# Token-major attention numerators, resident weights and small interleaved steps in a four-layer linear-attention and gated-MLP kernel

## Chip, cores and metric

The kernel runs on one core of one Trainium2 chip. The metric is the device time of one execution in microseconds (us). A time is a median over several executions.

Engines are named as in the profile: PE is the tensor engine, DVE the vector engine, ACT the scalar engine, POOL the GpSimd engine. SP issues most of the transfers (DMA).

## The reference

Two residual layers, A (linear attention with a "hedgehog" feature map) and B (a gated MLP), are applied twice: A, B, A, B. All data are bf16. There are S = 2048 tokens of D = 512 features, H = 32 heads of 16 features, and a hidden width F = 1376.

```python
def _A_ref(x, wqkv, w_phi, wo):                      # called on layernorm(x)
    q, k, v = split_heads(x @ wqkv)                  # cut: reshape and transpose to (b, h, s, 16)
    pq = einsum("bhsd,hdf->bhsf", q, w_phi)
    pk = einsum("bhsd,hdf->bhsf", k, w_phi)
    phi_q = concatenate([softmax(pq), softmax(-pq)], axis=-1)
    phi_k = concatenate([softmax(pk), softmax(-pk)], axis=-1)
    kv  = einsum("bhsf,bhsd->bhfd", phi_k, v)
    z   = einsum("bhsf->bhf", phi_k)
    num = einsum("bhqf,bhfd->bhqd", phi_q, kv)
    den = einsum("bhqf,bhf->bhq", phi_q, z)[..., None] + 1e-6
    return merge_heads(num / den) @ wo

def _B_ref(x, W_gate, W_up, W_down):                 # called on layernorm(x)
    return (relu(x @ W_gate) * (x @ W_up)) @ W_down

x = x + _A_ref(layernorm(x), ...); x = x + _B_ref(layernorm(x), ...)
x = x + _A_ref(layernorm(x), ...); x = x + _B_ref(layernorm(x), ...)
```

The important fact is that `kv` and `z` are sums over all tokens. No token's attention output can be computed before the last token's K and V are in. Each A layer therefore has two phases, a K/V phase and a query phase, with a barrier between them.

## The kernel before

The kernel records its operations one by one with what each reads and writes. A list scheduler in the kernel's own Python code then fixes the order on each engine, using an assumed duration per operation, and puts in the semaphore waits. The order on the chip is static: an instruction that has to wait holds up all that stand behind it on the same engine. Tokens are handled in 16 tiles of 128, or in 4 slabs of 512.

The layers are recorded one after the other. In the attention the query side is kept feature-major (features on the partitions, 512 tokens in the columns). Softmax sums and denominators then lie across partitions, so the kernel gets them with many small matmuls, takes reciprocals on DVE, transposes them on PE and spreads them again over the partitions with broadcast matmuls. Long lines are cut at `[...]`.

```python
for st in range(NSLAB):                 # softmax sums of q: 32 small matmuls a slab, 32 columns each
    for tt in range(4):
        for sg in range(2):
            for c in range(NC):
                op("pe", [...] e.matmul(zqv[:, tt, sg, :], expq[:, st, c, sg, tt*128:(tt+1)*128], EC2[:, c, :], [...]
    [...]                               # reciprocal, ratio R (DVE), 4 transposes (PE), copy (DVE)
    for c in range(NC):                 # R spread over partitions by a matmul of 512 columns
        op("pe", [...] e.matmul(pb[bk][:], EC[:, c, :], RT_sb[:, st*512:(st+1)*512], [...]
        [...]                           # expqm = expq * R, on POOL or DVE
[...]                                   # the same again for the denominators: 32 small matmuls, rden, transposes
for st in range(NSLAB):
    for c in range(NC):
        op("pe", [...] e.matmul(pb[nb][:], kvbd[:, 0, c, :], expq[:, st, c, 0, :], [...]      # numerator
        op("pe", [...] e.matmul(pb[nb][:], kvbd[:, 1, c, :], expqm[:, st, c, :], [...]        # numerator
        op("pe", [...] e.matmul(pb[rbb][:], EC[:, c, :], rdenT_sb[:, st*512:(st+1)*512], [...]  # 1/den spread
        [...]                           # oT = numerator * rdenb, POOL or DVE
    for tt in range(4):                 # output projection, residual on DVE
        [...]
```

The block-diagonal `kvbd` holds the 16x16 `kv` blocks of 8 heads on its diagonal, for a group of 128 features. DVE makes it from the sums in PSUM with a mask, 128 columns at a time, read and written in the same order:

```python
kvv = pb[bk][:, 0:136].rearrange("p (h e) -> p h e", e=17)
op("dve", [...] e.tensor_tensor(kvbd[:, sg, c, :].rearrange("p (h d) -> p h d", d=16), kvv[:, :, 0:16],
                                EC2[:, 0, 0:8].unsqueeze(2).to_broadcast([P, 8, 16]), ALU.mult) [...]
```

`kvbd` holds the 16x16 `kv` blocks of 8 heads on its diagonal. In the K/V phase, `vhat = v * 1/sum(exp(k))` is made on POOL or DVE for each sign of the feature map. The gated layer loads its weights (4.2 MB) into a region that shares its place with `vhat`, so they are loaded once for each gated layer:

```python
def layer_B(li, my_ln, next_ln):
    dma("sp", [...] Wg[:] [...]); dma("sp", [...] Wu[:] [...]); dma("sp", [...] Wd [...])
    for st in range(NSLAB):
        for fc in range(NFC):           # 11 column steps: 4 gate and 4 up matmuls of 512 columns,
            [...]                       # relu on ACT, product on DVE with "up" read from PSUM
        for tt in range(4):             # down projection: 11 matmuls of 512 columns a tile
            [...]
```

The softmax here doesn't subtract the row's maximum and nothing guards it: scores larger than these inputs give would overflow.

Of the kernel before, what the change touches and what calls it, by code (L numbers as in the profile page):

```python
# [45 lines left out]
class Program:  # L46
    SYNC_LAT = 500.0
# [222 lines left out]


class KB:

    def __init__(self, nc, A_x, A_wqkv, A_w_phi, A_wo, B_W_gate, B_W_up, B_W_down, out,
                 nlayers=4, debug_outs=None, dve_vhat_tiles=(2, 5, 7, 10, 13, 15), resid_on_pool=False, ot_mode="half", expqm_mode="half", nr_iters=1, ln_pre_emit=False, rstd_mode="dve", yt_copy_act="half", wcopy_act=True,
                 window=(("sp", 64), ("act", 96), ("pe", 300), ("dve", 24), ("pool", 32)), sched_params=(("SYNC_LAT", 500.0), ("SAME_LAT", 600.0))):
        self.dve_vhat_tiles = tuple(dve_vhat_tiles)
        self.resid_on_pool = resid_on_pool
        self.ot_mode = ot_mode
        self.expqm_mode = expqm_mode  # L280
        self.nr_iters = nr_iters
        self.ln_pre_emit = ln_pre_emit
        self.rstd_mode = rstd_mode
        self.yt_copy_act = yt_copy_act
        self.wcopy_act = wcopy_act
        self.nc = nc
        self.prog = Program(nc, window=dict(window))
        sp = dict(sched_params) if sched_params else {}
        if "SYNC_LAT" in sp:
            self.prog.SYNC_LAT = sp["SYNC_LAT"]  # L290
        if "SAME_LAT" in sp:
            self.prog.SAME_LAT = sp["SAME_LAT"]
        if "DMA_BW" in sp:
            self.prog.DMA_BW = sp["DMA_BW"]
        if "DMA_FIXED" in sp:
            self.prog.DMA_FIXED = sp["DMA_FIXED"]
        if "DMA_GLOBAL_Q" in sp:
            self.prog.DMA_GLOBAL_Q = sp["DMA_GLOBAL_Q"]
        self.A_x, self.A_wqkv, self.A_w_phi, self.A_wo = A_x, A_wqkv, A_w_phi, A_wo
        self.B_W_gate, self.B_W_up, self.B_W_down, self.out = B_W_gate, B_W_up, B_W_down, out  # L300
        self.debug_outs = debug_outs or {}
        self.nlayers = nlayers
        B, S, D = A_x.shape
        assert B == 1 and D == 512 and S % 512 == 0
        self.S = S
        self.NT = S // 128
        self.NSLAB = S // 512
        self.D = 512
        self.NC = 4
        self.H = 32  # L310
        self.DH = 16
        self.HF = 512
        self.F = B_W_gate.shape[1]
        assert self.F == 1376
        self.NFC = 11
        self.FLAST = self.F - 10 * 128
        self.eps_ln = 1e-5
        self.eps_den = 1e-6

    def op(self, eng, fn, reads=(), writes=(), dur=100.0, name=""):  # L320
        return self.prog.op(eng, fn, reads, writes, dur, name)

    def dma(self, eng, fn, reads=(), writes=(), nbytes=0, name=""):
        return self.prog.dma(eng, fn, reads, writes, nbytes, name)

    def build(self):
        nc = self.nc
        S, NT, NSLAB, NC, NFC = self.S, self.NT, self.NSLAB, self.NC, self.NFC
        with ExitStack() as ctx:
            E = ctx.enter_context  # L330
            self.sems = {e: E(nc.semaphore(f"sem_{e}")) for e in ENG_NAMES}
            self.dsems = [E(nc.semaphore(f"dsem{i}")) for i in range(self.prog.n_dma_sems)]

            x_sb = E(nc.sbuf_tensor("x_sb", [P, NT, 512], BF16))
            yT = E(nc.sbuf_tensor("yT", [P, NC, S], BF16))
            wv = E(nc.sbuf_tensor("wv", [P, NC, 512], BF16))
            Wqp = E(nc.sbuf_tensor("Wqp", [P, NC, 512], BF16))
            Wkp = E(nc.sbuf_tensor("Wkp", [P, NC, 512], BF16))
            wo_sb = E(nc.sbuf_tensor("wo_sb", [P, NC, 512], BF16))
            BD = E(nc.sbuf_tensor("BD", [P, NC, 128], BF16))  # L340
            ones_c = E(nc.sbuf_tensor("ones_c", [P, 4, 32], BF16))
            ident = E(nc.sbuf_tensor("ident", [P, 128], BF16))
            ident32 = E(nc.sbuf_tensor("ident32", [P, 128], FP32))
            EC2 = E(nc.sbuf_tensor("EC2", [P, 4, 32], BF16))
            EC2t = E(nc.sbuf_tensor("EC2t", [P, 4, 32], BF16))
            ones32 = E(nc.sbuf_tensor("ones32", [P, 4, 128], BF16))
            EC = E(nc.sbuf_tensor("EC", [P, 4, 128], BF16))
            eps_c = E(nc.sbuf_tensor("eps_c", [P, 1], FP32))
            stats6 = E(nc.sbuf_tensor("stats6", [P, NT, 6], FP32))
            mv = E(nc.sbuf_tensor("mv", [P, NT, 2], FP32))  # L350
            rstd = E(nc.sbuf_tensor("rstd", [P, NT, 1], FP32))
            rs_v1 = E(nc.sbuf_tensor("rs_v1", [P, NT, 1], FP32))
            rs_hx = E(nc.sbuf_tensor("rs_hx", [P, NT, 1], FP32))
# [45 lines left out]
            def RR(key):  # L399
                r = R.get(key)  # L400
                if r is None:
                    r = R[key] = Res(str(key))
                return r
# [504 lines left out]
```

## Time and profile before

| | before |
|---|---|
| median of 3 runs | 456.74 us (456.6 to 456.99) |
| span of the profiled run | 453.7 us |
| PE busy | 417.4 us, 92% |
| DVE, ACT, POOL busy | 298.8, 174.8, 92.8 us |
| first K/V matmul | 18.37 us |
| first matmul of gated layer 1 / 2 | 124.33 / 336.43 us |
| PE work at the warm rate (my sum, below) | about 401 us |

The page of the kernel before gives the span, the busy time of each engine, the busy share in 40 slices of 11.3 us each (in tenths), the granted PE clock in tenths, and at its end the chain of work that ended last, by engine.

```profile
span 453.7 us, 6812 instructions
...
PE 417.4 (92%) x2592; PEld 202.9 (45%) x2592; DVE 298.8 (66%) x696; ACT 174.8 (39%) x317; POOL 92.8 (20%) x128
...
PE   2598989899499999999999999989979999999997
...
DVE  4959984889974333368758999488997333343342
...
PEclk9999999999989999999999999999999999999999
...
PE 72%; DVE 18%; issue 3%; DMA 3%; ACT 2%; POOL 1%; SPq 1%; DVEq 0%; POOLq 0%
```

The PE row is at 9 nearly everywhere, so PE is the limit there. It dips in the first two slices, to 4 in the eleventh (113 to 125 us, the move from attention to the gated layer), and a little in the slices of the second attention layer. Where PE stands at 8 in the fourth, sixth and eighth slice, the DVE row stands at 9, 8 and 8: there DVE is about as busy as PE.

PE's busy spans overlap (matmuls are pipelined), so busy time is not a count of work. Work is better counted as the number of matmuls times their spacing. This is PE's timeline in the kernel before; the columns are start, duration, engine, line, operation, operands, count, and in brackets the idle time before it and what released it:

```profile
440.95 9.68 PE L794 MATMUL pb<-regB,regA 128*128 128x512 bf16 x44
```

44 matmuls of 512 columns take 9.68 us including the last one's latency; subtracting that latency gives 9.5 us, or 216 ns each. The Trainium skill ("TensorE: Matmul & The Clock Gate", Part 1: The HAM clock gate) states a spacing of columns / 2.4 GHz plus about 2.5 ns once the clock is warm, that is 215.7 ns for 512 columns; this trace agrees. With that rate the whole kernel before holds 1,696 matmuls of 512 columns (366 us), 256 of 136 columns (15), 512 of 32 columns (13) and some 7 us of transposes and setup: about 401 us. The 32-column matmuls stand 25 ns apart; in the line below, the matmul after these 24 starts at 66.06 us:

```profile
65.45 0.76 PE L665 MATMUL pb<-EC,expq 128*128 128x32 bf16 x24
```

The same timeline shows:

```profile
18.37 3.62 PE L604 MATMUL pb<-wv,yT 128*128 128x512 bf16 x8
```

The first V matmul starts only at 18.4 us. And at the first handover:

```profile
118.30 1.90 PE L748 MATMUL pb<-wo_sb,oT 128*128 128x512 bf16 x8 [0.93 <-DVE x_sb L757]
124.33 1.66 PE L779 MATMUL pb<-yT,regB 128*128 128x512 bf16 x4 [4.13 <-DMA yT<-ytile]
```

The last output projections (L748) wait 0.93 us for a bank to come free, and the gated layer's first matmul (L779) waits 4.13 us for a transposed tile. The largest waits of PE in the kernel before, with the total, the number and the longest:

```profile
PE pb L499 <- DMA regA<-in_A_wqkv_dram: 7.5, 2, 6.3
PE pb L779 <- DMA yT<-ytile: 5.8, 2, 4.1
PE pb L748 <- DVE x_sb L757: 5.3, 9, 1.4
```

The first is the load of the weights at the start, the second the handover, the third the output projection.

### The profile page before, as it was taken

What the parts mean: (1) busy time and instruction counts of PE and PEld (TensorE: products, weight loads), DVE (VectorE), ACT (ScalarE), POOL (GpSimd) and SP (SyncE); (2) the same over time, 40 slices, a digit from 0 to 9 for tenths busy, and PEclk for the clock granted to TensorE, in tenths of its full rate; (3) what the DMA queues carried; (4) which work ended last, traced back from release to release, by engine and by line L of the source; (5) the groups of instructions that cost most, each with busy time, mean ns of one, the idle gap of its engine ahead of it and who ended that gap; (6) DMA issues with size and microseconds to landing.
All of it is one profiled execution on the core that took longest, in us unless ns stands there. A gap on an engine that the chain in (4) does not pass through costs nothing.

```text
span 453.7 us, 6812 instructions
## 1 busy us (share of the span) xinstructions
PE 417.4 (92%) x2592; PEld 202.9 (45%) x2592; DVE 298.8 (66%) x696; ACT 174.8 (39%) x317; POOL 92.8 (20%) x128
## 2 busy tenths in 40 slices
PE   2598989899499999999999999989979999999997
PEld 1243458443144444444444345745324444444443
DVE  4959984889974333368758999488997333343342
ACT  3488864445022131231315986435513123131230
POOL 6008660654000000000002666056400000000000
PEclk9999999999989999999999999999999999999999
DMA  8752003610233000002220200370023210100101
GB/s 275 154 94 36 1 1 105 216 58 0 46 72 69 0 2 0 1 0 48 47 46 1 46 1 1 127 237 15 0 56 73 59 48 0 46 1 0 48 1 46
DMA packets 46800, 23.59 MB, mean 52 GB/s; under 512 B 35824, under 2 KB 44720, under 8 KB 46768
## 3 DMA queue, kind: packets, MB, share of 16 engines
q1 hardware_dynamic: 45184, 21.59, 18.6%
q10 hardware_dynamic: 1584, 1.57, 1.0%
q8 instruction: 20, 0.33, 0.3%
q14 instruction: 12, 0.10, 0.1%
HBM read 12.66 MB, written 2.10 MB: 33 GB/s over the span
## 4 chain that ended last, share of the span: by engine, by line
PE 72%; DVE 18%; issue 3%; DMA 3%; ACT 2%; POOL 1%; SPq 1%; DVEq 0%; POOLq 0%
PE pb L779 17%; PE pb L782 17%; PE pb L794 17%; PE pb L604 4%; PE pb L653 4%; PE pb L640 3%; DVE Zk L610 3%; DVE x_sb L757 3%; PE pb L602 2%; DVE regB L630 2%; PE pb L748 2%; DVE stats L530 2%; DMA BD<-in_A_w_phi_dram 2%; DVE expqm L684 1%; PE pb L665 1%
## 5 line engine op out<-in xcount | busy, mean ns | idle before, releaser
L785 ACT ACTIVATE gate_sb<-pb 128x512 bf16<-128x512 f32 (+1 forms) x88 | 52.5, 597 | 176.4 <-PE pb L779 155.8
L787 DVE TENSOR_TENSOR regA<-gate_sb,pb 128x512 bf16<-128x512 bf16 (+1 forms) x88 | 60.3, 686 | 71.4 <-PE pb L782 68.9
L779 PE MATMUL pb<-yT,regB 128*128 128x512 bf16 (+1 forms) x352 | 90.9, 382 | 5.8 <-DMA yT<-ytile 5.8
L782 PE MATMUL pb<-yT,regB 128*128 128x512 bf16 (+1 forms) x352 | 90.9, 382 | 0.0
L622 POOL TENSOR_TENSOR regB<-vsb,rZk 128x512 bf16<-128x512 bf16 x40 | 41.8, 1058 | 176.8 <-DVE rZk L613 162.5
L794 PE MATMUL pb<-regB,regA 128*128 128x512 bf16 (+1 forms) x352 | 77.4, 379 | 0.0
L779 PEld LDWEIGHTS pb<-yT,regB 128*128 128x128 bf16 (+1 forms) x352 | 35.3, 101 | 47.8 <-issue 7.8
L782 PEld LDWEIGHTS pb<-yT,regB 128*128 128x128 bf16 (+1 forms) x352 | 35.5, 101 | 41.3 <-issue 1.1
L794 PEld LDWEIGHTS pb<-regB,regA 128*128 128x128 bf16 (+1 forms) x352 | 34.3, 98 | 41.5
L796 DVE TENSOR_TENSOR x_sb<-x_sb,pb 128x512 bf16<-128x512 bf16 x32 | 22.0, 687 | 46.6 <-PE pb L794 46.6
L530 DVE BATCH_NORM_STATS2 stats<-x_sb 128x6 f32<-128x512 bf16 x64 | 42.5, 671 | 6.3 <-DMA x_sb<-in_A_x_dram 6.3
L656 ACT ACTIVATE expq<-pb 128x512 bf16<-128x512 f32 x64 | 35.7, 613 | 19.9 <-PE pb L653 17.9
L607 ACT ACTIVATE regA<-pb 128x512 bf16<-128x512 f32 x64 | 35.0, 612 | 17.5 <-PE pb L602 17.5
L604 PE MATMUL pb<-wv,yT 128*128 128x512 bf16 x128 | 35.5, 395 | 3.4 <-DVE regB L630 3.3
L610 DVE TENSOR_REDUCE Zk<-regA 128x64 f32<-128x1024 bf16 x32 | 37.8, 1188 | 1.1 <-ACT regA L607 1.1
L748 PE MATMUL pb<-wo_sb,oT 128*128 128x512 bf16 x128 | 32.8, 380 | 5.3 <-DVE x_sb L757 5.3
L602 PE MATMUL pb<-Wkp,yT 128*128 128x512 bf16 x128 | 34.0, 379 | 0.4 <-ACT Wqp L513 0.2
L653 PE MATMUL pb<-yT,Wqp 128*128 128x512 bf16 x128 | 33.5, 379 | 0.0
L577 DVE TENSOR_SCALAR ytile<-x_sb,mv,rstd 128x512 bf16<-128x512 bf16 x64 | 22.7, 406 | 5.6 <-DMA yT<-ytile 5.5
L690 POOL TENSOR_TENSOR expqm<-expq,rbt_sb 128x512 bf16<-128x512 bf16 x16 | 18.5, 1155 | 35.9 <-ACT rbt_sb L688 35.9
L733 ACT ACTIVATE rdenb_sb<-pb 128x512 bf16<-128x512 f32 x32 | 18.4, 597 | 13.8 <-PE pb L731 7.1
L739 POOL TENSOR_TENSOR oT<-rdenb_sb,numT_sb 128x512 bf16<-128x512 bf16 x16 | 18.5, 1155 | 21.9 <-ACT numT_sb L737 15.0
(75 smaller groups left out, 427.2 us busy)
## 6 DMA issues: line engine op xcount, KB each, us to landing
regB<-in_B_W_gate_dram SPq DMA_DIRECT2D x2, 1376.0 KB, 6.0
regB<-in_B_W_up_dram SPq DMA_DIRECT2D x2, 1376.0 KB, 6.0
regB<-in_B_W_down_dram SPq DMA_DIRECT2D x2, 1280.0 KB, 7.0
x_sb<-in_A_x_dram SPq DMA_DIRECT2D x4, 512.0 KB, 9.0
out_dram<-x_sb SPq DMA_DIRECT2D x3, 512.0 KB, 2.9
regA<-in_A_wqkv_dram ACTq DMA_DIRECT2D x2, 512.0 KB, 7.1
yT<-ytile SPq DMA_TRANSPOSE x64, 2.5
wv<-in_A_wqkv_dram ACTq DMA_DIRECT2D x1, 512.0 KB, 11.1
```

The costliest lines, as they stand in the source:

```text
L530: op("dve", (lambda t: (lambda e: e.bn_stats(stats6[:, t, :], x_sb[:, t, :])))(t), reads=[R_x[t]], writes=[R_stats[t]], dur=620, name=f"{t ...
L602: op("pe", (lambda t, ic, bk_k: (lambda e: e.matmul(pb[bk_k][:], yT[:, ic, t * 128:(t + 1) * 128], Wkp[:, ic, :], start=(ic == 0), stop=(i ...
L604: op("pe", (lambda t, ic, bk_v: (lambda e: e.matmul(pb[bk_v][:], yT[:, ic, t * 128:(t + 1) * 128], wv[:, ic, :], start=(ic == 0), stop=(ic ...
L610: op("dve", (lambda t, zb: (lambda e: e.tensor_reduce(Zk[:, zb, :], expk[:, t, :, :].rearrange("p s (h f) -> p (s h) f", f=16), AX.X, ALU. ...
L622: op("pool", (lambda vh, vb, rb, s: (lambda e: e.tensor_tensor(vh[:, :, 0:16], vsb[:, vb, :].rearrange("p (h d) -> p h d", d=16), rZk[:, r ...
L653: op("pe", (lambda st, c, ic, bk: (lambda e: e.matmul(pb[bk][:], Wqp[:, ic, c * 128:(c + 1) * 128], yT[:, ic, st * 512:(st + 1) * 512], st ...
L748: op("pe", (lambda tt, c, bk, ob: (lambda e: e.matmul(pb[bk][:], oT[:, ob, c, tt * 128:(tt + 1) * 128], wo_sb[:, c, :], start=(c == 0), st ...
L779: op("pe", (lambda st, fc, Mf, ic, gb: (lambda e: e.matmul(pb[gb][0:Mf, :], Wg[:, ic, fc * 128:fc * 128 + Mf], yT[:, ic, st * 512:(st + 1) ...
L782: op("pe", (lambda st, fc, Mf, ic, ub: (lambda e: e.matmul(pb[ub][0:Mf, :], Wu[:, ic, fc * 128:fc * 128 + Mf], yT[:, ic, st * 512:(st + 1) ...
L785: op("act", (lambda Mf, gb, gsb: (lambda e: e.activation(gate_sb[0:Mf, gsb, :], pb[gb][0:Mf, :], ACT.Relu)))(Mf, gb, gsb), reads=[R_pb[gb] ...
L787: op("dve", (lambda Mf, ub, gsb, hb, fc: (lambda e: e.tensor_tensor(hT[0:Mf, hb, fc, :], gate_sb[0:Mf, gsb, :], pb[ub][0:Mf, :], ALU.mult) ...
L794: op("pe", (lambda hb, fc, Kf, tt, bk: (lambda e: e.matmul(pb[bk][:], hT[0:Kf, hb, fc, tt * 128:(tt + 1) * 128], Wd[0:Kf, fc, :], start=(f ...
```

## The change

The intent is to take work off PE, and to let one layer's small operations run under the next layer's large matmuls.

1. **Token-major numerators.** Tokens lie on the partitions, and one matmul of 144 columns gives, for 128 tokens and a group of 8 heads, 128 numerator values, 8 denominators and 8 softmax sums. The normalisation is then six DVE operations per tile, with no broadcast matmul and no small transposes. A DMA transpose brings the tile back for the output projection.
2. **`phik` in place of `vhat`.** exp(k) is normalised in place on POOL, one operation of 1024 elements a tile.
3. **Resident weights.** The gated layers' weights have their own memory, and are loaded once, in pieces, during the first K/V phase.
4. **Small steps.** A gated slab is a list of 11 column steps and 4 down projections; steps of the attention (numerator, normalisation, layernorm of a tile) and of the next layer's K/V projection are emitted between them (`mix`). The first slab of each gated layer goes in two halves of 256 tokens, so that two finished tiles are enough to begin it.
5. **Start.** The first four tiles of x come one by one and are transposed on PE, and the reciprocal root of the layernorm is one POOL power operation.
6. **ACT copies.** In part of the first gated layer and the whole of the second, ACT copies "up" to SBUF, so that DVE's product reads no PSUM.

The diff is long (the file was rewritten). Its core, cut at `[...]`:

```diff
-            regA = E(nc.sbuf_tensor("regA", [P, nA], BF16))      # expk, hT and setup share this
-            regB = E(nc.sbuf_tensor("regB", [P, nB], BF16))      # vhat and the gated weights share this
+        sb("Wg", [NC, F])
+        sb("Wu", [NC, F])
+        sb("Wd", [NFC, 512])
+        sb("expk", [NT, 2, 512])
+        sb("kvbd", [NG, GW])                                     # 8 groups of 144 columns
-    vhat = v * rZk: two multiplies of 512 and two copies of 32 a tile, POOL or DVE [...]
+        op("pool", lambda e: e.tensor_tensor(                    # phik, in place
+            k.expk[:, t, :, :].rearrange("p s (h f) -> p (s h) f", f=16),
+            k.expk[:, t, :, :].rearrange("p s (h f) -> p (s h) f", f=16),
+            k.rZk[:, rb, :].unsqueeze(2).to_broadcast([P, 64, 16]), ALU.mult), [...]
+    def kv_fin(self, tag):                                       # kvbd, columns now ordered (d h)
+            op("dve", [...] e.tensor_tensor(
+                k.kvbd[:, g0:g0 + n, 0:128].rearrange("p g (d h) -> p g h d", h=8),
+                pv[:, :, 0:128].rearrange("p g (h d) -> p g h d", h=8),
+                k.mask8[:].unsqueeze(1).unsqueeze(3).to_broadcast([P, n, 8, 16]), ALU.mult) [...]
-    zq sums, Rtok, RbT, den, rden, rdenbT [...]                  # all of the feature-major query side
+    def num(self, t, nring, wring, tag):
+            for j in range(n):
+                op("pe", [...] e.matmul(k.pb[bank][:, j * GW:(j + 1) * GW],
+                    k.expq[:, st, c, s, tt * 128:(tt + 1) * 128], k.kvbd[:, g0 + j, :], [...]
+            op("act", [...] k.numbf[:, b, g0:g0 + n, :] [...])   # copy to SBUF as bf16
+        [...]                                                    # DVE: zm, zd, zr, ab, tsc, osb
+        self.dma_tr(lambda e: e.dma_start_transpose(k.oT[:, ob, :, :], k.osb[:, b, :]), [...]
+        for c in range(NC):                                      # output projection
+            op("pe", [...] e.matmul(k.pb[bank][:], k.oT[:, ob, c, :], k.wo_p[:, c, :], [...]
+            def mix(main, side):
+                n, m = len(main), len(side)
+                j = 0
+                for i, f in enumerate(main):
+                    while j < m and j * n <= i * m:
+                        side[j]()
+                        j += 1
+                    f()
+                for f in side[j:]:
+                    f()
+            N([0, 1, 2, 3])
+            for st in range(2 if not last else 1, NSLAB):
+                self.q_proj(st, qring, A)
+                mix(steps_B([0, 1], HA), steps_N([4, 5]))        # first slab in halves
+                mix(steps_B([2, 3], HA), steps_N([6, 7, 8]))
+                mix(steps_B(tiles(1), HA), steps_N([9, 10, 11, 12, 13]))
+                mix(steps_B(tiles(2)), steps_N([14, 15]) + steps_K(0))
+                mix(steps_B(tiles(3)), steps_K(1) + steps_K(2))  [...]
```

## The prediction

> **What bounds the kernel now.** The tensor engine (PE). The page: PE 92% busy of a 453.7 us span, DVE 66%, ACT 39%, POOL 20%; the chain of waits is 72% PE. Busy spans overlap, so I count work: in the timeline 44 down matmuls take 9.51 us (216 ns each), 96 KV matmuls of 136 columns 5.68 us (59 ns). Both fit the Trainium skill ("TensorE: Matmul & The Clock Gate", Part 1): columns / 2.4 GHz + about 2.5 ns once warm. 1,696 matmuls of 512 columns (366 us), 256 KV (15), 512 of 32 columns (about 16), transposes and setup (7): about 405 us. The other 49 us: first V matmul only at 18.4 us; DVE-bound K phases (DVE 10.0 of 10 us at 40-60, 260-280); attention-to-gated handovers (PE 7.4 and 5.9 of 10 us at 110-130, 8.9 at 320-330); 3 us of tail.
>
> **What changes.**
> - PE work removed: 512 small matmuls, 64 broadcasts (RbT, rdenbT), 64 numerators of 512 columns, 64 transposes: about 47 us. Added: 256 numerators of 144 columns, estimated 62.5 ns (16 us), and 16 transposes. First slab in halves: 352 matmuls of 256 columns, estimated 109 ns, +0.4 us. PE work falls about 31 us, to 374.
> - Start: per-tile x loads, K composed first, PE transposes. First K/V matmul at 12 us.
> - Handovers: two tiles suffice for the gated layer; N tiles and the second K/V projection run under gated matmuls; weights load once. The DVE-bound second K phase disappears there.
> - Moved: vhat becomes phik, all on POOL (estimate 2 x 1058 ns). In the first K phase POOL (34 us plus small LN work), ACT (48 us: exps, copies, applies) and DVE (16 x 1.73 + LN 13 = 41 us) stand near PE's 44. I expect 5-8 us more than PE needs.
> - DVE per N tile about 3.8 us (residual, stats, aggregate, apply measured 1.92; six new operations about 1.9, the bf16 ones estimated at the two-per-cycle rate of "VectorE: DVE Perf Modes", Mode 2x_1P; this trace has no such operation). Ten tiles, 38 us, fit under about 70 us of PE. In the last gated layer ACT copies "up", so the 0.69 us product should halve.
> - New chain per handover: numerator, copy, six DVE operations, DMA transpose (2.5 us now), output projection, LN, second transpose: about 15 us, partly filled by q projections. I expect 8 us of idle PE at each.
>
> **Sum.** 374 PE + 10 start + 7 K phase + 16 handovers + 3 tail = 410 at most, span about 408, time 2-3 us above: **410 us**, range 394 to 426. Faster by over 2%: 0.96; within 2%: 0.03; slower: 0.01.
>
> **What would show the steps.** First K/V matmul near 12 us; first gated matmul near 78 (now 124.3); second gated layer's first matmul near 270 (now 336.4). PE busy 380-390 us, about 94%; DVE near 290, ACT 245, POOL 120. PE idle lies in the first 80 us and some 15 us before the second gated layer; gated stretches over 97% PE. Numerators 62 ns apart; phik about 2.1 us.
>
> **What would make it wrong.** phik or the tiny POOL operations (power, per-tile scalars) slower, making POOL the limit of the first phase; weight pieces (4.7 MB) delaying DMA transposes there; the static order stalling PE inside gated stretches because chains of small operations run longer than its model; strided DVE operations (tsc, zm, ab) missing the fast mode. Full handovers: about 396.

## More of the kernel before

The busy times by stage (up to the first gated layer, from there to the second, the second gated layer; columns are length, then busy us and count of PE, PE weight loads, DVE, ACT and POOL, then the clock, the DMA share and GB/s):

```profile
0.00:124.33 124.33, 98.19 (x800) 51.49 (x801) 101.44 (x257) 66.38 (x123) 49.82 (x72) 1.00 0.34 90
124.33:336.43 212.10, 205.06 (x1264) 99.05 (x1265) 148.21 (x341) 82.14 (x150) 43.01 (x56) 0.99 0.16 41
336.43:450.70 114.27, 114.19 (x528) 52.36 (x528) 48.49 (x100) 26.25 (x44) 0.00 (x0) 1.00 0.12 32
```

The last gated layer is 114.27 us long and PE is busy for 114.19 us of it. Nothing but less PE work could shorten it. In the other two stages PE's busy time falls short by 26.1 and 7.0 us.

DVE makes `kvbd` in pieces of 128 columns (group lines give: line, engine, operation, output from inputs with shapes, count, then total busy us and mean ns, then idle time before it):

```profile
L643 DVE TENSOR_TENSOR kvbd<-pb,EC 128x128 bf16<-128x128 f32 x16 | 4.6, 290 | 8.9 <-PE pb L640 8.9
```

## The result and the profile after

The changed kernel takes 423.32 us (median of 4 runs, 422.99 to 423.9), against 456.87 us for the kernel before in the same rounds. The ratio is 0.9267, with a 95% interval of 0.9251 to 0.9283. Ratios in this document are the mean time of one kernel's fast runs over that of the other's fast runs of the same rounds, so they are not quite the ratio of the medians quoted. Where two changed kernels are compared that did not share rounds, I take the difference of their ratios to the kernel before, times 456.5 us.

The page of the kernel after, the same lines as before:

```profile
span 421.3 us, 6351 instructions
...
PE 390.8 (93%) x2336; PEld 209.9 (50%) x2336; DVE 283.5 (67%) x635; ACT 223.0 (53%) x455; POOL 117.5 (28%) x178
...
PE   4899985889979999999999999798999999999997
...
DVE  4999746886687578889665845786787758622222
...
PEclk9989998989999999999999999899999999999999
...
PE 80%; DVE 8%; DMA 5%; ACT 3%; POOL 2%; issue 1%; ACTq 0%; DVEq 0%; POOLq 0%
```

PE is busy 26.6 us less and its share is 93%. The chain is now 80% PE. PE's row dips in the first slice, to 5 in the seventh (63 to 74 us, the first handover), to 7 in the twelfth (116 to 126 us, inside the first gated layer), to 7 around 270 us (the second handover) and to 8 just after 284 us (the start of the second gated layer). The clock row has four 8s, where the row before has one.

PE's largest waits in the kernel after:

```profile
PE pb L552 <- DVE kvbd L526: 6.3, 2, 3.4
PE pb L421 <- DMA hT<-in_A_wqkv_dram: 5.3, 1, 5.3
PE pb L582 <- DMA oT<-osb: 3.3, 6, 1.1
...
PE pb L536 <- ACT expq L539: 2.6, 4, 1.3
PE pb L488 <- DMA yT<-ytile: 2.2, 1, 2.2
```

The first line is new. Twice, once per attention layer, PE waits for `kvbd`. These are the groups behind it, with other DVE operations for comparison:

```profile
L571 DVE TENSOR_TENSOR tsc<-numbf,ab 128x1024 bf16<-128x1024 bf16 x32 | 22.0, 687 | 0.6
...
L615 DVE TENSOR_TENSOR hT<-gate_sb,pb 128x512 bf16<-128x512 bf16 x25 | 17.1, 683 | 8.4 <-PE pb L603 7.4 <-PE pb L552 0.7
...
L612 DVE TENSOR_TENSOR hT<-gate_sb,expk 128x512 bf16<-128x512 bf16 x35 | 14.8, 424 | 30.0 <-ACT expk L610 29.8
...
L612 DVE TENSOR_TENSOR hT<-gate_sb,expk 128x256 bf16<-128x256 bf16 x30 | 8.3, 278 | 3.5 <-ACT expk L610 3.3
L521 DVE TENSOR_TENSOR kvbd<-pb,mask 128x384 bf16<-128x384 f32 x4 | 7.1, 1961 | 5.2 <-PE pb L510 5.2
...
L615 DVE TENSOR_TENSOR hT<-gate_sb,pb 128x256 bf16<-128x256 bf16 x10 | 4.1, 414 | 1.6 <-PE pb L603 1.5
...
L521 DVE TENSOR_TENSOR kvbd<-pb,mask 128x256 bf16<-128x256 f32 x2 | 2.6, 1292 | 0.0
```

The `kvbd` operation on 384 columns takes 1961 ns, and on 256 columns 1292 ns, so 5.2 ns per element (669 ns / 128). The other new DVE operations cost what I had estimated or a little more. `tsc` is 687 ns for 1024 elements. The product with both inputs in SBUF (L612) grows by 0.57 ns per element (424 against 278 ns, over 256 elements), against 1.05 ns for the product that reads PSUM (L615, 683 against 414). The Trainium skill ("VectorE: DVE Perf Modes", The perf-mode tier table) gives a two-source bf16 operation in SBUF twice the rate of one with a PSUM operand. This trace agrees on the slope, with a ratio of 1.84, but at 512 elements the whole operation is only 1.6 times faster (683 / 424), because a fixed part of about 130 ns stays.

PE's timeline at the first handover of the kernel after shows the wait itself, and the time around it:

```profile
65.11 0.64 PE L510 MATMUL pb<-vsb,expk 128*128 128x129 bf16 x8 [0.81 <-POOL expk L499]
69.12 0.36 PE L552 MATMUL pb<-kvbd,expq 128*128 128x144 bf16 x3 [3.38 <-DVE kvbd L526]
69.32 0.56 PE L536 MATMUL pb<-yT,Wqp 128*128 128x512 bf16 x1
...
86.91 1.01 PE L603 MATMUL pb<-yT,Wg 128*128 128x256 bf16 x4 [0.46 <-issue]
```

PE idles 3.38 us, and then a single q projection matmul (L536) takes 0.56 us, where one of the same shape takes 0.38 us at full clock (as at 67.15 us in the trace of run e1). The view by window says why (columns as before; the third number from the right is the clock):

```profile
68.00:69.00 1.00, 0.00 (x0) 0.00 (x0) 1.00 (x2) 0.00 (x0) 0.00 (x0) 1.00 0.00 0
69.00:70.00 1.00, 0.88 (x7) 0.62 (x8) 0.98 (x4) 0.48 (x1) 0.00 (x0) 0.69 0.00 0
70.00:71.00 1.00, 1.00 (x6) 0.40 (x4) 0.64 (x2) 0.58 (x2) 0.00 (x0) 0.50 0.00 0
```

After the idle stretch the granted clock goes to 0.5 at 69.4 us and stays there for 3.4 us. The Trainium skill ("TensorE: Matmul & The Clock Gate", Part 1) describes such half-rate stretches, in free-running windows of 3,413 ns. The clock records of this trace have four of them, at 21.6, 69.4, 86.4 and 267.4 us, each 3.4 us long (the four 8s of the clock row): 13.7 us at half rate, worth at most 6.8 us.

The stages of the kernel after:

```profile
0.00:86.91 86.91, 68.55 (x460) 37.10 (x461) 64.69 (x126) 60.45 (x114) 48.84 (x72) 0.96 0.48 124
86.91:284.13 197.22, 190.01 (x1118) 101.61 (x1119) 144.29 (x314) 92.98 (x193) 57.19 (x80) 0.98 0.17 33
284.13:418.20 134.07, 132.25 (x758) 71.20 (x758) 73.80 (x196) 69.61 (x150) 11.45 (x27) 1.00 0.19 42
```

### Where the time went

For each stage I subtract the PE work at the warm rate (matmul count times spacing) from the time that passed.

| part | before: lost | after: lost |
|---|---|---|
| start | to first gated matmul: 35.8 | 8.5 (0 to 10.55 us) |
| first K/V phase | (in the line above) | 9.1 (55.1 long, 46.0 work) |
| first handover | (in the line above) | 10.5 (21.3 long, 10.8 work) |
| gated layer 1 with the mixture | gated 1 to gated 2: 13.2 | 5.3 (154.7 long, 149.4 work) |
| second K/V phase's end | (in the line above) | 1.6 |
| second handover | (in the line above) | 6.1 |
| gated layer 2 | 0.3 | 3.1 (134.1 long, 131.0 work) |
| tail | 3.0 | 3.1 |
| **lost** | **about 52** | **47.3** |
| **work** | **about 401** | **374.0** |
| **span** | **453.7** | **421.3** |

So about 27 of the 32 us came from the PE work that was taken away, and about 5 us from less loss; most of the loss only lies elsewhere now. These are net sums. They do not say that the small steps are idle: without the halves (e4) or the hand-placed steps (e5) the time is 14 and 5 us longer, so they keep the new chain of small operations from using up the gain.

### The profile page after: what moved, and what is told of

Its sections match the earlier page's. It is cut to its first block, busy times and chain, and to the rows that moved or that the text cites. A ratio compares the mean times of both kernels' runs of the same rounds, so it can differ in the third digit from the quotient of the medians.

```text
span 421.3 us, 6351 instructions
## 1 busy us (share of the span) xinstructions
PE 390.8 (93%) x2336; PEld 209.9 (50%) x2336; DVE 283.5 (67%) x635; ACT 223.0 (53%) x455; POOL 117.5 (28%) x178
## 3 DMA queue, kind: packets, MB, share of 16 engines
q10 hardware_dynamic: 1584, 1.07, 0.9%
## 4 chain that ended last, share of the span: by engine, by line
PE 80%; DVE 8%; DMA 5%; ACT 3%; POOL 2%; issue 1%; ACTq 0%; DVEq 0%; POOLq 0%
PE pb L603 35%; PE pb L627 18%; PE pb L488 11%; PE pb L582 6%; PE pb L536 4%; DMA oT<-osb 3%; PE pb L510 3%; PE pb L552 3%; DVE kvbd L521 2%; POOL expk L499 1%; DMA phi_c<-in_A_w_phi_dram 1%; DVE tsc L571 1%; ACT expk L491 1%; DVE x_sb L584 1%; DVE stats L459 1%; DMA yT<-ytile 1%
## 5 line engine op out<-in xcount | busy, mean ns | idle before, releaser
L603 PE MATMUL pb<-yT,Wg 128*128 128x512 bf16 (+3 forms) x440 | 97.0, 339 | 0.6 <-issue 0.5
L603 PE MATMUL pb<-yT,Wu 128*128 128x512 bf16 (+3 forms) x440 | 97.2, 338 | 0.0
L605 ACT ACTIVATE gate_sb<-pb 128x512 bf16<-128x512 f32 (+3 forms) x110 | 56.1, 513 | 74.1 <-PE pb L603 68.5
L627 PE MATMUL pb<-Wd,hT 128*128 128x512 bf16 (+1 forms) x352 | 80.8, 379 | 0.5 <-DVE x_sb L629 0.4
L499 POOL TENSOR_TENSOR expk<-expk,rZk 128x1024 bf16<-128x1024 bf16 x32 | 61.5, 1928 | 38.0 <-DVE rZk L498 27.0
L556 ACT ACTIVATE numbf<-pb 128x432 bf16<-128x432 f32 (+1 forms) x96 | 44.3, 497 | 40.4 <-PE pb L552 38.5
L603 PEld LDWEIGHTS pb<-yT,Wu 128*128 128x128 bf16 (+1 forms) x440 | 43.9, 101 | 31.9
L603 PEld LDWEIGHTS pb<-yT,Wg 128*128 128x128 bf16 (+1 forms) x440 | 43.2, 101 | 32.2 <-issue 1.4
L496 DVE TENSOR_REDUCE Zk<-expk 128x64 f32<-128x1024 bf16 x32 | 38.4, 1204 | 21.8 <-ACT expk L491 21.8
L612 DVE TENSOR_TENSOR hT<-gate_sb,expk 128x512 bf16<-128x512 bf16 (+3 forms) x73 | 25.8, 354 | 36.8 <-ACT expk L610 36.5
L536 PE MATMUL pb<-yT,Wqp 128*128 128x512 bf16 x128 | 36.8, 401 | 3.2 <-ACT expq L539 2.6
L462 POOL TENSOR_TENSOR rstd<-rv,mhalf 128x1 f32<-128x1 f32 x64 | 37.2, 584 | 4.2
```

Of the source, the lines that this page charges most:

```text
L496: op("dve", lambda e: e.tensor_reduce(k.Zk[:, zb, :], k.expk[:, t, :, :].rearrange("p s (h f) -> p (s h) f", f=16), AX.X, ALU.add), [r("ex ...
L499: op("pool", lambda e: e.tensor_tensor(k.expk[:, t, :, :].rearrange("p s (h f) -> p (s h) f", f=16), k.expk[:, t, :, :].rearrange("p s (h ...
L536: op("pe", (lambda c, ic, bank: lambda e: e.matmul(k.pb[bank][:], k.Wqp[:, ic, c * 128:(c + 1) * 128], k.yT[:, ic, st * 512:(st + 1) * 512 ...
L556: op("act", (lambda g0, n, bank: lambda e: e.activation(k.numbf[:, b, g0:g0 + n, :], k.pb[bank][:, 0:n * GW].rearrange("p (g m) -> p g m", ...
L603: op("pe", (lambda bank, W, ic, fc, Mf: lambda e: e.matmul(k.pb[bank][0:Mf, 0:n], W[:, ic, fc * 128:fc * 128 + Mf], k.yT[:, ic, c0:c0 + n] ...
L605: op("act", (lambda Mf, gb, gs: lambda e: e.activation(k.gate_sb[0:Mf, gs, 0:n], k.pb[gb][0:Mf, 0:n], ACT.Relu))(Mf, gb, gs), [self.RP[gb] ...
```

## The experiments

Two questions were open.

- **Where did the gain come from?** My theory: from less PE work, so PE work added back costs nearly its whole length, wherever it is put. The rival: from better hiding of the handovers, so that PE has slack and added work costs less.
- **Why 13 us more than predicted?** My theory: the `kvbd` operation, which is not in the prediction, and the half-rate stretch that its wait sets off. Rivals: the clock drops by themselves, whatever makes PE idle; weight loads in the first K/V phase that delay the transposes; a static order that is wrong because its assumed durations are.

Each experiment is one edit of the changed kernel (e7 to e12: of e1's kernel). All outputs are right. e1 to e4, e5 to e8 and e9 to e12 each ran on one chip, with the kernel before in the same rounds (medians 456.54, 455.93 and 456.08 us).

| run | median us | ratio to before (95%) | against the changed kernel |
|---|---|---|---|
| changed kernel | 423.32 | 0.9267 (0.9251–0.9283) | |
| e1_kvread | 415.00 | 0.9085 (0.9064–0.9105) | −8.3 |
| e2_wo_twice | 448.79 | 0.9829 (0.9799–0.9859) | +25.7 |
| e3_filler | 427.26 | 0.9349 (0.9321–0.9377) | +3.7 |
| e4_whole_slab | 436.93 | 0.9567 (0.9535–0.9598) | +13.7 |
| e5_no_mix | 428.93 | 0.9382 (0.9344–0.9421) | +5.2 |
| e6_no_act_up | 424.85 | 0.9309 (0.9284–0.9333) | +1.9 |
| e7_kvread_wolate | 418.03 | 0.9174 (0.9149–0.9198) | −4.2 |
| e8_kvread_gatefill | 415.03 | 0.9102 (0.9077–0.9126) | −7.5 |
| e9_kvread_again (e1's kernel) | 415.06 | 0.9102 (0.9088–0.9116) | −7.5 |
| e10_kvread_model | 415.19 | 0.9116 (0.9089–0.9143) | −6.9 |
| e11_kvread_wdlate | 415.09 | 0.9098 (0.9072–0.9123) | −7.7 |
| e12_kvread_all | 417.90 | 0.9159 (0.9140–0.9178) | −4.9 |

Differences of less than about 1.5 us between kernels of different chips are not to be read: e1 and e9 are the same kernel, and their ratios differ by 0.8 us.

### e1_kvread: `kvbd` walked in the order of its writes

The `kvbd` operation walks heads outside and features inside, reading PSUM in order and writing SBUF with a stride of 8 bf16, 16 bytes. The edit turns the walk around: writes in order, PSUM reads with a stride of 16 fp32, 64 bytes. The values are the same, and the order of PE's instructions is the same as in the changed kernel.

```diff
-                k.kvbd[:, g0:g0 + n, 0:128].rearrange("p g (d h) -> p g h d", h=8),
-                pv[:, :, 0:128].rearrange("p g (h d) -> p g h d", h=8),
-                k.mask8[:].unsqueeze(1).unsqueeze(3).to_broadcast([P, n, 8, 16]), ALU.mult))(g0, n, pv),
+                k.kvbd[:, g0:g0 + n, 0:128].rearrange("p g (d h) -> p g d h", h=8),
+                pv[:, :, 0:128].rearrange("p g (h d) -> p g d h", h=8),
+                k.mask8[:].unsqueeze(1).unsqueeze(2).to_broadcast([P, n, 16, 8]), ALU.mult))(g0, n, pv),
```

> The kernel after, with one change: the permutation in the write of the block-diagonal KV matrix is moved from the write (bf16 at a stride of 8 elements in SBUF) to the read (fp32 at a stride of 16 elements in PSUM); every engine's order is unchanged. Theory A (the strided write is what makes this operation 1.96 us and the first handover wait long): the 128x384 operation falls to 0.5-0.7 us, PE's wait for it before the first numerators falls from 3.4 and 3.0 us to about 1.5 and 1, the half-rate clock after it goes, and the time falls by 4 to 7 us, to 416-419. Rival B (the cost lies in reading PSUM or in the broadcast mask, or the handover is bound further down by the chain through two DMA transposes): the operation stays above 1.5 us, or it falls and the time moves by less than 1.5 us.

Measured: 415.00 us (412.74 to 415.7), 8.3 us less than the changed kernel, more than the 4 to 7 us expected. The groups of e1:

```profile
L521 DVE TENSOR_TENSOR kvbd<-pb,mask 128x384 bf16<-128x384 f32 x4 | 2.0, 552 | 5.2 <-PE pb L510 5.2
...
L521 DVE TENSOR_TENSOR kvbd<-pb,mask 128x256 bf16<-128x256 f32 x2 | 0.8, 415 | 0.0
```

1961 ns has become 552, and the slope is 1.07 ns per element, about that of an ordinary PSUM read above (1.05). So the strided PSUM read costs nothing that can be seen, and the strided SBUF write cost a factor of five. (The edit also changes the order in which the mask is read: before it, each mask value is repeated in the inner loop. That is not the cause, because the kernel before reads its mask in that way too, with writes in order, and takes 290 ns for 128 columns, L643 above.) The Trainium skill ("SBUF — State Buffer", Door 1: The DMA port swizzle, the note on cachelines) says that each access that crosses into a new 16-byte line pays a penalty. The write stride here is just such a line, and the direction agrees; the page gives no figure. PE's timeline of e1 at the same place:

```profile
63.82 0.64 PE L510 MATMUL pb<-vsb,expk 128*128 128x129 bf16 x8 [0.81 <-POOL expk L499]
65.38 0.77 PE L552 MATMUL pb<-kvbd,expq 128*128 128x144 bf16 x6 [0.92 <-DVE kvbd L526]
...
81.49 1.01 PE L603 MATMUL pb<-yT,Wg 128*128 128x256 bf16 x4 [0.32 <-issue]
```

The wait for `kvbd` is 0.92 us in place of 3.38, and no half-rate stretch follows it. PE's waits for `kvbd` fall from 6.3 to 1.4 us in all. Over both handovers the lost time falls from 16.6 to 8.4 us. The waits explain 4.9 of these 8.2 us. The two half-rate stretches that followed the waits in the changed kernel are gone in e1; at half rate over 3.4 us each is worth 1.7 us, together 3.4, and 4.9 + 3.4 = 8.3. The trace divides the time in the same way. From the last K/V-sum matmul to the first numerator 3.59 and 3.60 us pass in the changed kernel, and 1.14 and 1.13 us in e1; from there to the first gated matmul 17.79 and 17.75 us, and in e1 16.11 and 15.99, 1.7 and 1.8 us less, with the same order on PE. So the sum fits in both its parts, but no run changes the clock alone (e3 was to do so).

e1 beats both kernels, and no later run beats it by more than the noise.

### e2_wo_twice: PE work put back

```diff
-        for c in range(NC):
+        for c in list(range(NC)) * 2:
             op("pe", (lambda c, bank: lambda e: e.matmul(k.pb[bank][:], k.oT[:, ob, c, :], [...]
```

Each output projection runs twice. The accumulation starts anew at each `c == 0`, so the second pass overwrites the first and the output stays correct. It adds 32 tiles x 4 matmuls x 215.7 ns = 27.6 us of PE work, in small portions, all in the query phases and under the gated layers.

> The kernel after, with each output projection done twice (128 more matmuls of 512 columns, 27.6 us of PE work at 216 ns; results unchanged). Theory A (PE work is the limit wherever attention tiles run under gated matmuls, so removed PE work is gained one for one): 24 of 32 tiles lie there, 20.7 us; with a part of the 8 others, time plus 21 to 27 us, 444-450. Rival B (those stretches hang on DVE and ACT chains that PE waits for): less than plus 12 us.

Measured: 448.79 us, +25.7 us, 93% of the added work and inside the 21 to 27 us expected. PE has next to no slack in the stretches where these projections lie, so the theory that the gain is mostly the removed work stands, and the rival falls. Some 2 us of it may have been hidden in waits. e2 tests the changed kernel only: that the removed work cost its full length in the kernel before is the count above and not a run.

### e3_filler: keep PE busy in the `kvbd` wait

```diff
     def kv_fin(self, tag):
         op, r, k = self.op, self.r, self
+        for i in range(14):
+            op("pe", lambda e: e.matmul(k.pb[7][:], k.wv_p[:, 0, 0:128], k.Wkp[:, 0, :], start=True, stop=True),
+               [r("wv", 0), r("wk", 0)], [self.RP[7]], 216, f"{tag} fill {i}")
```

14 matmuls whose results nobody reads (3.0 us) are recorded where PE waits for `kvbd`. They were to leave the wait's cause and take away the idle time that sets off the half rate.

> The kernel after, with 14 useless matmuls of 512 columns (3.0 us at the full clock) put on PE just before each wait for the block-diagonal KV matrix. Theory A (the half-rate clock after each idle stretch costs time): PE clock 1.0 after both waits instead of 0.5 for some 3.2 us, and 1 to 3 us less in all, 420-422. Rival B (PE is not what the handover waits for, the chain over ACT, DVE and DMA is): clock 1.0 there but the time within 1 us of 423.3.

Measured: 427.26 us (423.57 to 428.22, 6 runs), +3.7 us, which neither side expected. PE's timeline of e3 at the second handover shows why this settles nothing (L518 is the filler, L555 the numerator):

```profile
260.10 2.75 PE L518 MATMUL pb<-Wkp,wv_p 128*128 128x512 bf16 x12
...
266.71 0.56 PE L555 MATMUL pb<-kvbd,expq 128*128 128x144 bf16 x6 [2.09 <-DVE kvbd L529]
```

The scheduler moved the filler. Twelve of the 14 matmuls run ahead of the last eight K/V-sum matmuls (262.69 to 263.10 us), on which `kvbd` depends; in the first handover all 13 that the trace holds do. So PE still waits 2.52 and 2.09 us for `kvbd`, and from the first gated matmul to the last K/V-sum matmul 178.5 us pass, against 175.9 in the changed kernel. The half-rate time is 13.7 us as before, but at 83.7 to 90.5, 268.0 and 288.5 us. This experiment failed to fill the wait, and so to separate the wait from the half rate. Filler placed in this way is no remedy.

### e4_whole_slab: the first slab not in halves

```diff
-                mix(steps_B([0, 1], HA), steps_N([4, 5]))
-                mix(steps_B([2, 3], HA), steps_N([6, 7, 8]))
+                mix(steps_B(tiles(0), HA), steps_N([4, 5, 6, 7, 8]))
```

The same is done in the second gated layer, where the steps are 4 to 9.

> The kernel after, with the first gated slab whole (512 columns) and not in halves, so the gated layer waits for four attention tiles. Theory A (halves let the gated layer start about two tiles earlier, at about 3 to 4 us of chain per tile): first gated matmul at 90-94 us instead of 86.9, and in the second layer likewise; time plus 4 to 10 us, 427-433. Rival B (the other work fills that time): within 1.5 us of 423.3.

Measured: 436.93 us, +13.7 us, more than the 4 to 10 us expected. One of its four runs was over 1.5% above the fastest and is not in the ratio; the median of the other three is 435.77 us. PE's timeline of e4:

```profile
99.84 1.02 PE L603 MATMUL pb<-yT,Wg 128*128 128x512 bf16 x4 [2.55 <-DMA yT<-ytile]
```

The gated layer now begins at 99.84 us after a wait of 2.55 us for a transposed tile, 12.9 us later than in the changed kernel. Its clock records show 30.7 us at half rate in place of 13.7 us; (30.7 − 13.7) / 2 = 8.5 us would be the most that this is worth. So the halves are a large part of the change: the gated layer can begin with two tiles and need not wait for four. How the 13.7 us divide between plain idle time and the slower clock is not shown by this run.

### e5_no_mix: no small steps in the emission order

```diff
             def mix(main, side):
+                for f in side:
+                    f()
+                side = []
                 n, m = len(main), len(side)
```

The attention steps are recorded ahead of the gated steps rather than between them. The scheduler is unchanged and may still move instructions past each other, within a window of 400 PE and 40 DVE operations.

> The kernel after, with the attention tiles (and the second K/V tiles) of each group emitted before the column steps of the gated layer instead of in small steps between them; the list scheduler still reorders inside its windows (PE 400 operations, DVE 40). Theory A (the small steps are what keeps PE fed: a tile takes DVE about 4 us but PE only 1.4 us): PE idles in the gated stretches, time plus 10 to 30 us, 433-453. Rival B (the scheduler's windows find the same mixture): within 3 us of 423.3.

Measured: 428.93 us, +5.2 us, between what the two sides expected (10 to 30, and within 3). The gated layers still begin at 88.3 and 285.8 us, against 86.9 and 284.1. So the scheduler finds most of the interleaving itself, and placing the steps by hand is worth some 5 us, a small part of the 33.

### e6_no_act_up: ACT does not copy "up"

```diff
-            HA = range(NFC) if last else range(0, NFC, 2)
+            HA = ()
```

> The kernel after, with the up-projection always read by DVE from PSUM (0.68 us per 512 columns) and never copied by ACT first (then 0.42 us). DVE gains 11.6 us of work in the last gated layer (33 x 0.26 + 22 x 0.14) and about 3 us in the first, ACT loses 36 us. Theory A (DVE has slack under gated matmuls, so this moves little): within 3 us of 423.3. Rival B (DVE is near the limit where attention tiles run, so its work counts): plus 5 to 12 us, 428-435.

Measured: 424.85 us, +1.9 us, hardly more than the noise between chips. DVE has room in the gated layers either way. The prediction's step "the 0.69 us product should halve" was about an operation that is off the critical path (it fell to 0.42 us).

### e7_kvread_wolate: weight pieces later and packed

In the first K/V phase of e1 PE waits about 2.1 us for a transposed tile near 20 us. The guess was that the first weight pieces delay that transpose. The edit sends no piece with the second slab's tiles, and three with each tile after that, in place of two throughout.

```diff
-                    for _ in range(2):
+                    for _ in range(0 if st == 0 else 3):
                         if pieces:
                             pieces.pop(0)(self.r("rstd", t))
```

> The first run's kernel (read-side permutation), with the weight pieces held back until the transposes of tiles 4 to 7 are issued (none at those four tiles, then three per tile). Theory A (the wo pieces issued on the same queue delay the first DMA transposes by about 1-2 us, and the 2.1 us wait of PE at 19-21 us with the clock drop after it comes from that): that wait falls below 1 us and the first gated matmul comes 1 to 3 us earlier than 81.5; time 412-414 beside 415.0. Rival B (the K phase is bound by POOL and ACT anyway): the wait goes but the first gated matmul stays within 1 us of 81.5 and the time within 1 us of 415.

Measured: 418.03 us, about 4 us slower than e1 (3.3 us against e9, the same kernel as e1 in other rounds). The wait near 20 us is 2.19 us still, though no weights are under way by then: the guess was wrong. What came instead is in PE's waits of e7:

```profile
PE pb L488 <- DMA yT<-ytile: 7.1, 3, 4.0
```

With the pieces packed three to a tile, a transpose keeps PE waiting 4.0 us at 50 us, and the total for these waits is 7.1 us against 3.6 in e1. So packed weight loads seem to delay transposes. As e1 spaces them they do little near 20 us; whether they have a part in e1's second wait (1.50 us at 24.6 us, 0.91 at 32.6 us in e7) is not shown.

### e8_kvread_gatefill: filler ahead of the gated layer

In e1 one half-rate stretch is left, at 80.6 us, just as the first gated layer begins. The edit puts six matmuls that nobody reads ahead of it.

```diff
+            for i in range(6):
+                self.op("pe", lambda e: e.matmul(self.pb[4][:], self.wv_p[:, 0, 0:128], self.Wkp[:, 0, :], start=True, stop=True),
+                        [self.r("wv", 0), self.r("wk", 0)], [self.RP[4]], 216, f"{A} gatefill {i}")
             if last:
                 mix(steps_B([0, 1], HA), steps_N([4, 5, 6]))
```

> The first run's kernel, with six useless matmuls of 512 columns (1.3 us) on PE between the last attention tile of a handover and the first gated matmul, to keep the clock up through the thin stretch there (PE idle 79.4-81.5 us). Theory A (half-rate clock on the first 3.4 us of gated matmuls costs 1.7 us): no half-rate stretch after the handover, time 413 to 414 beside 415.0. Rival B (the clock drop only moves to another thin stretch, as the filler of the third run made it do): half-rate time stays at 3.4 us or more, time within 1 us of 415.

Measured: 415.03 us, as e1. PE's timeline of e8:

```profile
82.18 0.60 PE L603 MATMUL pb<-yT,Wg 128*128 128x256 bf16 x4
...
85.65 1.04 PE L582 MATMUL pb<-wo_p,oT 128*128 128x512 bf16 x4 [1.45 <-DMA oT<-osb]
```

Four matmuls of 256 columns take 0.60 us here and took 1.01 us in e1: the clock is full in e8. But PE then waits 1.45 us for the output projection's transposed tile, and the stretch up to the end of gated layer 1 is 154.6 us long, against 154.5 us in e1. A PE that ran ahead arrives early at a wait that something else ends. The half rate at this place costs nothing that can be seen.

### e9_kvread_again: e1's kernel once more

This is e1's kernel without an edit, beside e10 to e12 on their chip.

> The first run's kernel again, as the base for the other runs of this set on the same chip. Expected as before: ratio to the kernel before 0.906 to 0.911, about 415.

Measured: 415.06 us. The profiled span is 414.3 us, against 411.0 in e1. 2.6 us of these 3.3 have arisen by 14.5 us, and the later waits of the K/V phase agree to 0.02 us (one is 2.13 us at 20.29 us in e1, and 2.12 us at 22.85 us in e9). PE's timeline of e9:

```profile
11.07 2.34 PE L488 MATMUL pb<-wv_p,yT 128*128 128x512 bf16 x5
```

and of e1:

```profile
10.15 1.24 PE L488 MATMUL pb<-wv_p,yT 128*128 128x512 bf16 x5
```

Five matmuls of 512 columns take 2.34 us in e9 and 1.24 us in e1, so PE is cold (at half rate) there in e9. Yet the view by window of e9 has 1.00 in the clock column in this stretch:

```profile
11.00:12.00 1.00, 1.00 (x4) 0.37 (x3) 1.00 (x4) 0.00 (x0) 0.18 (x1) 1.00 1.10 348
```

This 1.00 is not a record. The trace's first clock record begins at 14.42 us in e9 and at 8.91 us in e1, and the view prints 1.00 where there is none; in e9 the slow spacing ends where the record begins. The Trainium skill ("TensorE: Matmul & The Clock Gate", Part 1, its note on the warm-up budget) says that the number of cold matmuls at the start varies from run to run. This is seen here, in two runs of the same kernel. So two single spans of one kernel can differ by 2 to 3 us for this reason.

### e10_kvread_model, e11_kvread_wdlate, e12_kvread_all: three refinements

Gated layer 1 still loses about 5 us in e1, and the first K/V phase about 8. On e1's kernel, e10 tries a cause for the first (durations assumed in the scheduler that are too short), e11 one for the second (the last weight pieces), and e12 both with another order of the q projection's PSUM banks, so that the first of them need not wait for the K/V banks. The lines for e10 sum up its diff.

```diff
 e10: durations set to those of the trace
-  hT product 75 + n * 0.52, osb 340, zm and ab 190, zd 150, zr 330, layernorm apply 407
+  hT product 132 + n * 0.57, osb 418, zm and ab 219, zd 188, zr 347, layernorm apply 469
 e11: the six pieces of Wd only after the first kv_fin
-                        if pieces:
+                        if len(pieces) > 6:
 [...]
         self.kv_fin("A0")
+        for f in pieces:
+            f(self.r("kvbd", 0))
 e12: both, and
-            qring, gring, dring = cycle([0, 1, 2, 3]), cycle([0, 1, 2, 3]), wring
+            qring, gring, dring = cycle([3, 0, 1, 2]), cycle([0, 1, 2, 3]), wring
```

> The first run's kernel, with the durations that its list scheduler assumes for seven DVE operations set to the measured ones (bf16 product 424 ns for 512 columns where 341 was assumed, o 418 for 340, zm and ab 219 for 190, zd 188 for 150, zr 347 for 330, apply 469 for 407); only orders change. Theory A (the idle of PE inside the gated stretches, some 8 us in all, comes from an order that was made with too short chains): PE's waits for numbf and oT in the stretches fall, time 1 to 4 us below the base. Rival B (the order is as good as it gets, or the stretches lose time for other reasons): within 1 us of the base.

> The first run's kernel, with the down-projection weights (1.4 MB) loaded only after the first K phase, when the DMA engines are idle (share 0.00 at 60-70 us). Theory A (weight loads delay the DMA transposes of the K phase, as 4 us of waiting did in the seventh run, where they were packed more tightly): last KV accumulation 1 to 2 us earlier than 64.5, time 1 to 2 us below the base. Rival B (in this order the loads are hidden, PE waits for transposes only at 20-25 us, where few weights are under way): within 1 us of the base.

> The first run's kernel with both of the last two changes, and the ring of PSUM banks of the later q projections begun at bank 3, so that the first of them need not wait for the KV banks to be read. If both theories hold and add up: 3 to 6 us below the base, 409-412; if neither does, within 1.5 us of it.

Measured against e9 in the same rounds: 415.19 (e10), 415.09 (e11) and 417.90 us (e12), where e9 has 415.06. The first two make no difference, the third is 2.8 us slower. None of the three edits wins anything back. In e10 gated layer 1 takes 154.8 us (85.7 to 240.5 us), as in e9. So these seven assumed durations are not the cause; wrong durations are a risk that the prediction had named. The loss stays unexplained.

## Why the prediction was right, and where it was not

The prediction was 410 us with a range of 394 to 426; 423.32 us lies inside the range, near its upper end. Its sum, term by term, against the profiled run:

| term of the prediction | predicted us | measured us |
|---|---|---|
| "374 PE" | 374 | 374.0 |
| "10 start" | 10 | 8.5 |
| "7 K phase" | 7 | 9.1, and 1.6 in the second K/V phase |
| "16 handovers" | 16 | 16.6 (10.5 + 6.1) |
| gated stretches (no term) | 0 | 8.4 (5.3 + 3.1) |
| "3 tail" | 3 | 3.1 |
| span | 410, then "about 408" | 421.3 |

**Right: the mechanism and its largest number.** The prediction counted work and not busy time, and its 374 us after the change are what the trace holds. e2 shows that this work limits the changed kernel: work put back costs 93% of its length. The work before was counted too high, by 3 to 4 us, mostly because the 512 small matmuls stand 25 ns apart and not 31. So PE work fell by 27 us and not 31. The lost time was to fall from 49 to 36 us, and fell from 52 to 47. Together these two are why a gain of 47 us was predicted and 33.5 came.

**Right by compensation: the handovers.** 16 us were predicted and 16.6 measured, but not for the reasons given. The prediction did not foresee the strided `kvbd` write, which cost about 8 us over the two handovers (e1). Without it they lose 8.4 us. So the chain from numerator to second transpose, which I had put at 8 us of idle PE each, is hidden better than I thought, and the two errors cancelled by luck. The prediction named strided operations as a risk, but it named `tsc`, `zm` and `ab`. These took about what was estimated (0.69, 0.22 and 0.22 us; the six new operations take 2.08 us together against an estimate of 1.9). The operation that was slow was one that seemed to be moved unchanged: 290 ns for 128 columns before, with writes in order. Its layout had changed to feature-outside, head-inside.

**Wrong, the step that failed: "gated stretches over 97% PE".** As a statement about the profile it is right: PE is busy for 98.3% of the first gated layer and 98.6% of the second. But it was then put into the sum as zero loss, although 2 to 3% of 289 us is 6 to 9 us. Measured: 8.4 us. Here belongs the half clock too, which the prediction left out of the sum altogether. e8 and e9 show that in e1's kernel it costs next to nothing in gated layer 1: e9 has no half-rate stretch there and takes 154.8 us, e1 has one and takes 154.5 us. e10 rules out the seven assumed durations that it changed. Of the 5.1 us lost there in e1, PE's timeline shows 2.4 us as visible waits: 0.43 and 0.50 us for ACT's copies of the numerators, 1.07 us for the transposed attention tile, and 0.41 us for a residual. The changed kernel has the same four. The first three lie within 6 us of each other, which is the 7 in the twelfth slice of its PE row. I read them as a chain of small operations that ran longer than the PE work placed over it; no run tests this. The rest stays open.

**Mis-sized: the K/V phase.** I expected 5 to 8 us in the first phase and no DVE-bound second one; measured are 9.1 and 1.6 us. The parts that can be seen in the first are one wait of 2.2 us for a transpose, the half-rate stretch that starts with it at 21.6 us (3.4 us long, so about 1.7 us), and waits of 1.25, 0.37 and 0.81 us for ACT and POOL at its end.

**The milestones.** The first K/V matmul came at 10.6 us (predicted 12), the first gated matmul at 86.9 (78), and the second gated layer at 284.1 (270). PE busy is 390.8 us (380–390 predicted, about 94%; measured 93%), DVE 283.5 (290), ACT 223.0 (245), POOL 117.5 (120). `phik` takes 1.93 us (2.1 predicted).

**Not tested.** Resident weights alone, in the old structure; the feature-major query side in the new structure; and a `kvbd` that is contiguous on both sides. How many of e1's 8.3 us were the half clock and how many the wait is supported by a sum and not shown by a run.

## What to carry to other kernels

When PE is the limit, count matmuls times their measured spacing, before and after. The count after the change was exact here; the count before was 3 to 4 us off, mostly where one spacing had not been measured. What was said of waits was a guess: at the handovers its errors happened to cancel, in the gated layers they did not. And remember that a stretch that is "98% busy" still loses its 2% in a sum of hundreds of microseconds. When an operation is carried over into a new layout, look at the stride of its writes anew, above all when it stands at a barrier: here one five-line operation of 2 us, run three times per layer, cost 8 us, and turning its loop around gave them back.

## What the Trainium skill lacked or had wrong

- "SBUF — State Buffer", the note on cachelines: it names a penalty per 16-byte line but no figure. ("Vector Engine (DVE) Microarchitecture Reference", 5.2, has figures for streams of 4-byte words in SBUF that step by 24 words and more, but none for a bf16 write.) Here a DVE operation that writes bf16 with a stride of 16 bytes takes 5.2 ns per element (1961 ns for 384), against 1.07 ns per element with writes in order (552 ns).
- The same page and "PSUM — Partial Sum Buffer" warn of non-contiguous PSUM access, for matmuls; neither says what a DVE read of PSUM with a stride costs. Here reading fp32 from PSUM with a stride of 64 bytes costs nothing visible: 1.07 ns per element, against 1.05 ns for an ordinary read (L615).
- "TensorE: Matmul & The Clock Gate", Part 1, gives at least one idle window of about 3.4 us as the condition for half rate, and does not say how idle it must be. Here the length of a single gap does not decide. In the 3.4 us before the four drops of the changed kernel PE was busy for 1.24, 0.26, 1.58 and 0.97 us. In e1 a gap of 2.13 us near 20 us lies across two such windows (15.74 to 19.15 and 19.15 to 22.56 us, by its clock records), with 2.42 and 2.27 us of busy time, and the clock stayed full. I cut all 14 traces into these windows: of those at the full clock, every one that PE filled to less than 0.41 was followed by half rate (16), none over 0.53 was, and of the 26 between, 13 were.
- No page says that a trace can lack clock records at its start: in e9 the first one begins at 14.42 us, and in the kernel before at 22.18 us, while matmuls of 512 columns stand some 426 ns apart before it. A view that prints 1.00 there misleads.
